# The seven-expert search counted by TensorE, the weights' second halves made on VectorE, and one expert to a turn in the smaller rounds

## The chip, the cores and the metric

The kernel runs on one NeuronCore of a Trainium2 chip. The metric is the device time of one execution in microseconds (us); lower is better. The engines are named as in the profile: PE is TensorE (PEld its weight loads), DVE is VectorE, ACT is ScalarE, POOL is GpSimd, SP the queue of plain DMAs.

## The reference

Three stages follow each other: a two-dimensional Fourier transform, a mixture of eight experts with a greedy assignment, and a dense feed-forward layer.

```
X = fft(fft(x, axis=1), axis=2).real            # x is 8 x 3072 x 256
logits = X.reshape(24576, 256) @ w_gate         # 8 experts, each takes at most 3072 tokens
for (token, e) in order of falling logits:
    if token is free and e is not full: assign token to e
out[tokens of e] = relu(X[tokens of e] @ w1[e]) @ w2[e]
result = (max(h, 0) + alpha * min(h, 0)) @ w_out    with h = out @ w_in
```

## The kernel before

The transform runs first (the first 445 us). It leaves the transformed rows in DRAM (`XD`) and the logits in SBUF (`LG`, 128 partitions x 192 columns x 8 experts).

The greedy assignment is worked out in **rounds**. Each round finds the expert that fills up first, and with it the logit at which it does: a search over a 32-bit key, the upper 16 bits first and the lower 16 after. The tokens that this expert has won are written to a list, the logits of the remaining experts are moved together (`place`), and the next round goes on with one expert fewer. The first list, with all eight experts (`first`, `count_wide`), is made before the feed-forward part starts. Rounds 1 to 7, with n = 7 down to 1 experts, are made while the feed-forward part works on earlier lists.

A search step before (`round`, inner function `search`, L725 to L750) settles two bits. For each of the n experts three DVE instructions (`junk`, L732) count how many of the 192 keys of a partition reach a threshold; one small matmul (`cnt`, L723) sums over partitions; a few DVE instructions choose the digit and subtract it from the keys. Sixteen steps make a search of 32 bits.

The feed-forward part takes 48 **tiles** of 512 tokens, six for each list. A tile is four layers: `l1` (tile name `h`), `l2` (`y`), `l3` (`u`) and `l4` (`o`), the last two one tile behind the first two. PE is given them in 48 **parts** a tile, in a fixed order: eight groups, each of one `l1`, two `l3`, two `l4` and one `l2` part. Every product is made three times with numbers cut into a first half (fp32r) and a remainder, so each part's result is taken from PSUM by ACT (first half) and then DVE (remainder): `hs`, `r` and `g`, `ys`, `xtl`. After each part's matmuls the loop asks the router for its next piece (`next(bg, None)`), and only then emits what takes the part's result out. I call each such call a **turn**: what the router emits in a turn stands on DVE ahead of the part's own remainder. The router's `lag()` lets two turns pass before it puts a matmul on PE. Every engine runs its instructions in this written order.

Before an expert's tiles begin, its eight weight blocks are fetched, and `place_w` cuts each into `wxh` (ACT, L820) and the remainder `wxl` (POOL, L821). Six blocks are placed in the last tile of the expert before, the last two in the first two groups of the expert's own first tile. These first tiles, 6, 12, 18, 24, 30, 36 and 42, are called **switches** below. POOL's queue also holds the gathers of token rows (`xg`) and the scatters of results (`out_dram`).

If a list is not ready when the loop needs it (the gather of the next list's first tile, in group 5 of the tile before), the loop empties turns one after another with no part between them. Round 1 comes to this in tile 5.

Of the kernel before, what the change touches and what calls it, by code (L numbers as in the profile page):

```python
# [10 lines left out]
F32 = mybir.dt.float32  # L11
F32R = mybir.dt.float32r
BF16 = mybir.dt.bfloat16
I32 = mybir.dt.int32
I16 = mybir.dt.int16
U16 = mybir.dt.uint16
F16 = mybir.dt.float16
AF = mybir.ActivationFunctionType
ALU = mybir.AluOpType
AX = mybir.AxisListType  # L20
# [3 lines left out]
P = 128  # L24
B, N, D = 8, 3072, 256
E = 8
TOK = B * N
N1, N2 = 96, 32
NG = 24
HC = 138  # L30
CV = 256
NCOL = TOK // P
# [236 lines left out]
class Router:  # L269
# [395 lines left out]
    def rank(self, n):  # L665
# [24 lines left out]
                yield  # L690
        yield

    def round(self, psum, lists, n):

        nc, wp = self.nc, self.wp
        V = nc.vector
        if n == 1:
            at = wp.tile([P, 2, NCOL], BF16, tag="at", name="at")
            V.tensor_scalar(at[:, 0], self.done, 0.0, None, op0=ALU.is_equal)
            V.memset(at[:, 1], 0.0)  # L700
            V.tensor_copy(self.estar, self.eid[:, :1])
            yield "expert"
            yield from self.place(psum, lists, at, n)
            return
        yield from self.rank(n)
        ke = wp.tile([P, E - 1, NCOL], U16, tag="ke", name="ke")
        s = wp.tile([P, E - 1, 3], BF16, tag="s", name="s")
        junk = [wp.tile([P, NCOL], BF16, tag="w", bufs=2, name="junk") for _ in range(2)]

        def keys(k16):  # L710

            for e in range(0, n, 4):
                m = min(n, e + 4)
                V.tensor_tensor(
                    ke[:, e:m], k16[:, None, :].broadcast_to([P, m - e, NCOL]), self.ohe[:, e:m], op=ALU.mult
                )
                yield

        def total(k):

            cnt = psum(name="cnt")
            cv = cnt[:, : n * k].rearrange("p (e k) -> p e k", e=n)
            nc.tensor.matmul(cv, self.onesb[:, :P], s[:, :n, :k], start=True, stop=True)  # L723
            return cv

        def search():
            step = 65536
            while step > 1:
                step >>= 2
                for e in range(n):  # L730
                    for k in range(3):
                        V.tensor_scalar(  # L732
                            junk[(e + k) % 2], ke[:, e], float((k + 1) * step), 0.0, op0=ALU.is_ge, op1=ALU.add,
                            accum_out=s[:, e, k : k + 1],
                        )
                    if e % 2:
                        yield
                yield from self.lag()
                cv = total(3)
                yield  # L740
                mc = wp.tile([P, 3], F32, tag="mc", name="mc")
                V.tensor_reduce(out=mc, in_=cv.rearrange("p e k -> p k e"), op=ALU.max, axis=AX.X)
                st = wp.tile([P, 3], F32, tag="st", name="st")
                V.memset(st, float(step))
                nk = wp.tile([P, 1], F32, tag="nk", name="nk")
                V.scalar_tensor_tensor(mc, mc, self.CAP, st, op0=ALU.is_ge, op1=ALU.mult, accum_out=nk)
                if step > 1:
                    V.tensor_scalar(ke[:, :n], ke[:, :n], nk, 0.0, op0=ALU.subtract, op1=ALU.max)
                V.tensor_tensor(self.base, self.base, nk, op=ALU.add)
                yield  # L750

        k16 = wp.tile([P, NCOL], U16, tag="k16b", name="k16b")
        V.tensor_scalar(k16, self.hi, 32768.0, 0.0, op0=ALU.add, op1=ALU.max)
        V.memset(self.base, 0.0)
        yield from keys(k16)
        yield from search()
        V.tensor_scalar(self.base, self.base, -32768.0, None, op0=ALU.add)
        key = self.low_key()
        V.memset(self.base, 0.0)
        yield  # L760
        V.tensor_scalar(key, key, 32768.0, None, op0=ALU.add)
        V.tensor_scalar(k16, key, 0.0, 65535.0, op0=ALU.max, op1=ALU.min)
        yield from keys(k16)
        yield from search()

        for e in range(n):
            V.scalar_tensor_tensor(
                junk[e % 2], key, self.base, self.ohe[:, e], op0=ALU.is_ge, op1=ALU.mult, accum_out=s[:, e, :1]
            )
            yield  # L770
        yield from self.lag()
        cv = total(1)
        yield
        we = wp.tile([P, E], F32, tag="we", name="we")
        V.scalar_tensor_tensor(we[:, :n], cv[:, :, 0], self.CAP, self.wE[:, :n], op0=ALU.is_ge, op1=ALU.mult)
        V.tensor_reduce(out=self.wm, in_=we[:, :n], op=ALU.max, axis=AX.X)
        V.scalar_tensor_tensor(
            we[:, :n], we[:, :n], self.wm, self.eid[:, :n], op0=ALU.is_equal, op1=ALU.mult, accum_out=self.estar
        )
        yield  # L780
        at = self.choose(key)
        yield "expert"
        yield from self.place(psum, lists, at, n)
# [6 lines left out]
def ffn_phase(tc, XD, wcat, W3S, alpha, out, router):  # L790
    nc = tc.nc
    with ExitStack() as ctx:
# [25 lines left out]

        def split_w(dh, dl, raw):
            nc.scalar.copy(dh, raw)  # L820
            nc.gpsimd.tensor_sub(dl, raw, dh.bitcast(F32))  # L821

        st = {}

        def new_lists(r):
            lm = lp.tile([P, 2, NG], F32, tag="lm", name=f"lm{r}")
            idx = lp.tile([P, NG], I32, tag="idx", name=f"idx{r}")
            st["lists", r] = (lm, idx)
            return lm, idx
# [19 lines left out]
        def place_w(r, i):  # L849
            split_w(wxh[i], wxl[i], raws.pop((r, i)))  # L850
# [189 lines left out]
        with tc.tile_pool(name="r_first", bufs=1) as fp:  # L1040
            i = None
            first = router.first(psum_r, new_lists(0), fp)
            for tag in first:
# [5 lines left out]
                if tag == "expert":  # L1049
                    expert_idx(0)  # L1050
                    i = 0
# [15 lines left out]
        op = ctx.enter_context(tc.tile_pool(name="m_o", bufs=3))  # L1067
# [166 lines left out]
```

## Time and profile before

| | us |
|---|---|
| median of 3 runs (3885.62 to 3892.1) | 3889.99 |
| the profiled execution | 3883.63 |
| its span, first to last instruction | 3881.9 |
| PE busy | 3788.3 (98%) |
| PEld busy | 3327.8 (86%) |
| DVE busy | 2611.5 (67%) |
| ACT busy | 1815.8 (47%) |
| POOL busy | 657.7 (17%) |

The profiled execution lies 6.4 us under the median. Busy time is the time in which at least one instruction of the engine runs; matmuls overlap, and their ends are modelled, so PE's 98% is no statement on how well it is used. What can be read from it is where PE stands idle.

### The profile page before, as it was taken

The numbers are of one execution on the slowest core, as the hardware profiler recorded it, in microseconds if no ns is written. First come the engines' busy times: TensorE is split into PE (matmuls) and PEld (weight loads), VectorE is DVE, ScalarE is ACT, GpSimd is POOL, SyncE is SP. The second block draws the span as 40 slices with busy tenths as digits, with TensorE's granted clock in tenths as the row PEclk, the third lists the DMA queues.
The fourth block names the chain that finished last, engine by engine and source line by source line (L and its number), as shares of the span: only waits on it lengthen the run. The fifth ranks groups of instructions, "written<-read, shape, count | busy, mean of one in ns | idle before, by whom it ended". The sixth has DMA issues, their size and how long they took to land.

```text
span 3881.9 us, 62378 instructions
## 1 busy us (share of the span) xinstructions
PE 3788.3 (98%) x23666; PEld 3327.8 (86%) x23676; DVE 2611.5 (67%) x7650; ACT 1815.8 (47%) x3455; POOL 657.7 (17%) x905
## 2 busy tenths in 40 slices
PE   9999899999999999999999999999999999999999
PEld 8998587888888788888888888888888888888888
DVE  5776899689868977887877777556444444444444
ACT  4553244444444444454444444454445444544444
POOL 2211300030011110030011110030112201211010
PEclk9999899999999999999999999999999999999999
DMA  8786100010000000010000000010001000100000
GB/s 235 203 218 199 44 12 12 10 40 12 12 23 23 23 23 12 12 44 12 12 23 23 22 23 12 12 44 12 14 20 33 22 12 22 29 16 22 12 17 12
DMA packets 95053, 153.53 MB, mean 40 GB/s; under 512 B 14688, under 2 KB 64544, under 8 KB 94752
## 3 DMA queue, kind: packets, MB, share of 16 engines
q0 software_dynamic: 30400, 90.21, 7.8%
q1 hardware_dynamic: 63440, 58.75, 5.5%
q8 instruction: 185, 3.03, 0.3%
q14 instruction: 116, 0.95, 0.1%
q10 hardware_dynamic: 912, 0.58, 0.1%
HBM read 90.77 MB, written 58.72 MB: 39 GB/s over the span
## 4 chain that ended last, share of the span: by engine, by line
PE 83%; DVE 13%; issue 2%; ACT 1%; DMA 1%; POOL 0%; SPq 0%; ACTq 0%; POOLq 0%; DVEq 0%
PE o L998 24%; PE u L918 23%; PE y L918 12%; PE h L918 11%; DVE junk L732 5%; PE b L209 4%; PE a L150 3%; DVE r L971 2%; PE ls L659 2%; PE c L226 2%; DVE g L976 2%; PE xps L908 1%; DVE hs L932 1%; DMA x<-in_x 1%; ACT r L969 1%
## 5 line engine op out<-in xcount | busy, mean ns | idle before, releaser
L998 PEld LDWEIGHTS o<-w3t,g 128*128 128x128 f32 x9216 | 1178.8, 188 | 92.3 <-DVE g L976 30.7
L998 PE MATMUL o<-w3t,g 128*128 128x256 f32 x9216 | 1209.5, 281 | 27.2 <-DVE g L976 25.2
L918 PE MATMUL u<-ys,w3t 128*128 128x512 f32 x4608 | 1183.7, 394 | 0.2 <-DVE ys L954 0.2
L971 DVE SCALAR_TENSOR_TENSOR r<-a,nal,r 128x512 f32<-128x512 f32 x768 | 597.3, 778 | 623.2 <-ACT a L970 620.7
L918 PEld LDWEIGHTS u<-ys,w3t 128*128 128x128 f32 x4608 | 841.6, 189 | 160.7 <-DVE ys L954 1.2
L969 ACT ACTIVATE r<-u 128x512 f32<-128x512 f32 x768 | 459.4, 598 | 847.9 <-PE u L918 668.4
L1021 POOL DMA_INDIRECT out_dram<-os,orow x192 | 190.0, 989 | 2594.3 <-ACT os L1017 2526.0
L931 ACT ACTIVATE hs<-h 128x512 fp32r<-128x512 f32 x384 | 230.3, 600 | 779.5 <-PE h L918 756.0
L976 DVE TENSOR_TENSOR g<-r,g 128x512 fp32r<-128x512 f32 x768 | 526.7, 686 | 4.3
L932 DVE SCALAR_TENSOR_TENSOR hs<-h,hs 128x512 fp32r<-128x512 f32 x384 | 264.5, 689 | 380.2 <-ACT hs L931 379.9
L918 PE MATMUL y<-hs,wxh 128*128 128x512 f32 x1536 | 490.3, 400 | 0.6 <-DVE hs L932 0.6
L975 ACT CAST g<-r 128x512 fp32r<-128x512 f32 x768 | 477.8, 622 | 22.9 <-DVE r L971 22.9
L970 ACT ACTIVATE a<-u 128x512 f32<-128x512 f32 x768 | 454.9, 592 | 0.0
L732 DVE TENSOR_SCALAR_CACHE_REDUCE junk<-ke 128x192 bf16<-128x192 uint16 x1296 | 367.5, 348 | 0.1
L918 PEld LDWEIGHTS y<-hs,wxh 128*128 128x128 f32 x1536 | 283.9, 189 | 61.2 <-DVE hs L932 1.0
L918 PE MATMUL h<-xth,wxh 128*128 128x512 f32 x768 | 304.0, 396 | 1.9 <-DVE hs L932 1.8
L918 PE MATMUL y<-hs,wxl 128*128 128x512 f32 x768 | 303.6, 395 | 0.0
L918 PE MATMUL h<-xtl,wxh 128*128 128x512 f32 x768 | 301.0, 392 | 0.2 <-DVE xtl L913 0.2
L918 PE MATMUL h<-xth,wxl 128*128 128x512 f32 x768 | 300.1, 391 | 0.0
L892 POOL DMA_INDIRECT xg<-XD,idx x192 | 207.3, 1080 | 85.0 <-issue 55.8
L918 PEld LDWEIGHTS y<-hs,wxl 128*128 128x128 f32 x768 | 144.4, 188 | 35.1
L918 PEld LDWEIGHTS h<-xth,wxl 128*128 128x128 f32 x768 | 144.5, 188 | 32.3
(227 smaller groups left out, 3641.5 us busy)
## 6 DMA issues: line engine op xcount, KB each, us to landing
x<-in_x SPq DMA_DIRECT2D x63, 384.0 KB, 4.8
XD<-xs SPq DMA_DIRECT2D x96, 128.0 KB, 2.8
XD<-xs SPq DMA_DIRECT2D x184, 64.0 KB, 2.7
raw<-in_w POOLq DMA_DIRECT2D x32, 256.0 KB, 4.4
W3S<-hl POOLq DMA_DIRECT2D x32, 256.0 KB, 3.2
w3t<-W3S SPq DMA_DIRECT2D x16, 512.0 KB, 9.6
tw<-in_tw POOLq DMA_DIRECT2D x12, 512.0 KB, 6.1
xg<-XD,idx POOLq DMA_INDIRECT x192, 2.8
```

Of the source, the lines that this page charges most:

```text
L732: V.tensor_scalar(junk[(e + k) % 2], ke[:, e], float((k + 1) * step), 0.0, op0=ALU.is_ge, op1=ALU.add, accum_out=s[:, e, k : k + 1],)
L892: nc.gpsimd.indirect_dma_start(out=x[:, j, :], out_offset=None, in_=XD, in_offset=bass.IndirectOffsetOnAxis(ap=idx[:, j0 + j : j0 + j + 1] ...
L918: nc.tensor.matmul(o, w, a, start=(first and n == 0), stop=(last and n == 2))
L931: nc.scalar.activation(h[:, 0], ps, AF.Relu)
L932: nc.vector.scalar_tensor_tensor(h[:, 1], ps, 0.0, h[:, 0].bitcast(F32), op0=ALU.max, op1=ALU.subtract)
L969: nc.scalar.activation(r, ps, AF.Relu)
L970: nc.scalar.activation(a, ps, AF.Relu, scale=-1.0)
L971: nc.vector.scalar_tensor_tensor(r, a, nal[:, j : j + 1], r, op0=ALU.mult, op1=ALU.add)
L975: nc.scalar.copy(g[:, 0], r)
L976: nc.vector.tensor_sub(g[:, 1], r, g[:, 0].bitcast(F32))
L998: nc.tensor.matmul(o[:, s, :], a, w, start=(j == 0 and n == 0 and s % 2 == 0), stop=(j == 15 and n == 2 and s % 2 == 1), skip_group_check= ...
L1021: ins = nc.gpsimd.indirect_dma_start(out=out, out_offset=bass.IndirectOffsetOnAxis(ap=orow[:, jj : jj + 1], axis=0), in_=os[:, s, :], in_o ...
```

## The change

Three things are changed. In the round with seven experts (round 1) the search is made by a new function, `search_beside`: it settles four bits a step, in eight steps. DVE makes a table of 15 comparisons for every key (`ind`, in three pieces a step), PE counts by multiplying the table with the experts' membership (`d`, 24 matmuls a step), and a last matmul sums (`cnt`). In rounds 3 to 6 (n under 6) the search ends a turn after every expert instead of after every second one. And `wxl` is written by DVE instead of POOL, in every place.

```diff
+    def search_beside(self, psum, n):
...
+                def ind(h):
+                    t = wp.tile([P, H, 16, 8], BF16, tag="ol", bufs=2, name="ind")
...
+                    V.tensor_tensor(
+                        t[:, :, first:k], blocks(key)[:, s, None, :].broadcast_to(sh),
+                        lows[:, i, None, 16 - k + first :, :].broadcast_to(sh), op=ALU.is_ge,
+                    )
+                    inds[h] = t
+
+                def products(h):
+                    t = inds.pop(h)
+                    for c in range(H):
+                        a = (h * H + c) * 8
+                        nc.tensor.matmul(
+                            dv, t[:, c, :k].rearrange("p k j -> p (k j)"), self.ohe[:, :n, a : a + 8],
+                            start=(h + c == 0), stop=(h == 2 and c == H - 1),
+                        )
+
+                ind(0)
+                yield
+                ind(1)
+                yield from self.lag()
+                d = psum(name="d")
+                dv = d[:q, : 8 * n].rearrange("p (e c) -> p e c", e=n)
+                products(0)
+                yield
+                ind(2)
+                products(1)
+                yield
+                yield from self.lag()
+                products(2)
+                yield
+                V.tensor_tensor(dm[:q, :n], dv, self.mske[:q, None, :].broadcast_to([q, n, 8]), op=ALU.mult)
+                s = wp.tile([P, E], F32, tag="we", name="se")
+                V.tensor_reduce(out=s[:q, :n], in_=dm[:q, :n], op=ALU.add, axis=AX.X)
+
+                V.scalar_tensor_tensor(
+                    s2[:q, :n, :k], s[:q, :n, None].broadcast_to([q, n, k]), -1536.0,
+                    self.mskj[:q, None, :k].broadcast_to([q, n, k]), op0=ALU.add, op1=ALU.mult,
+                )
+                yield from self.lag()
+                cnt = psum(name="cnt")
+                cv = cnt[:, : n * k].rearrange("p (e k) -> p e k", e=n)
+                nc.tensor.matmul(cv, self.ones[:q], s2[:q, :n, :k], start=True, stop=True)
+                yield
...
+                V.scalar_tensor_tensor(
+                    mc[:, :k], mc[:, :k], cap, st[:, :k], op0=ALU.is_ge, op1=ALU.mult, accum_out=nk
+                )
+                if i:
+                    nxt = wp.tile([P, NCOL], I16, tag="cur", bufs=2, name="cur")
+                    V.tensor_scalar(nxt, key, nk, -32768.0, op0=ALU.subtract, op1=ALU.max)
+                    key = nxt
+                V.tensor_tensor(self.base, self.base, nk, op=ALU.add)
+                yield
...
     def round(self, psum, lists, n):
...
         yield from self.rank(n)
+        if n == E - 1:
+            key = yield from self.search_beside(psum, n)
+            at = self.choose(key)
+            yield "expert"
+            yield from self.place(psum, lists, at, n)
+            return
...
-                    if e % 2:
+                    if e % 2 or n < 6:
                         yield
...
         def split_w(dh, dl, raw):
             nc.scalar.copy(dh, raw)
-            nc.gpsimd.tensor_sub(dl, raw, dh.bitcast(F32))
+            nc.vector.tensor_sub(dl, raw, dh.bitcast(F32))
```

How the change moves instructions is shown at three places. The first is PE in the search of round 1, tile 2; `cnt`, `d`, `h`, `u`, `y` and `o` are named as above, the numbers tell buffers apart. Before, the only matmul of the search is `cnt`:

```order
L918 MATMUL h_1_7170<-xth_7061,wxl_5171 128x512
L723 LDWEIGHTS onesb
L723 MATMUL cnt<-s,onesb 128x21
L918 MATMUL u_2_7182<-ys_7083,w3t_5148 128x512 x6
L998 MATMUL o_7205<-w3t_5146,g_0_7167 128x256 x12
L918 MATMUL u_3_7224<-ys_7083,w3t_5149 128x512 x6
```

With the change, eight matmuls `d`, each with its own weights, follow a part three times a step:

```order
L765 LDWEIGHTS ones
L765 MATMUL cnt<-lows,ones 128x105
L1043 MATMUL u_6_7356<-ys_7061,w3t_5152 128x512 x6
...
L1043 MATMUL h_4_7433<-xth_7039,wxl_5174 128x512
L735 LDWEIGHTS ind
L735 MATMUL d<-oh,ind 120x56
L735 LDWEIGHTS ind
L735 MATMUL d<-oh,ind 120x56
```

So PE gets 24 groups of eight `d` in round 1 and eight `cnt` instead of sixteen.

The second place is DVE in the same search. Before, runs of `junk` counts stand between the parts' own `hs`, `r` and `g`:

```order
L732 TENSOR_SCALAR junk,s<-ke 128x192 x6
L971 SCALAR_TENSOR_TENSOR r_13_6925<-a_13_6926,nal,r_13_6925 128x512
L976 TENSOR_TENSOR g_12_6930<-r_12_6884,g_12_6930 128x512
L732 TENSOR_SCALAR junk,s<-ke 128x192 x15
L932 SCALAR_TENSOR_TENSOR hs_7_6973<-h_7_6963,hs_7_6973 128x512
```

With the change, a piece of the table or three small instructions stand there:

```order
L725 TENSOR_TENSOR ind<-cur,lows 128x8x120
L1096 SCALAR_TENSOR_TENSOR r_11_6824<-a_11_6825,nal,r_11_6824 128x512
L1101 TENSOR_TENSOR g_10_6829<-r_10_6778,g_10_6829 128x512
L1057 SCALAR_TENSOR_TENSOR hs_6_6865<-h_6_6850,hs_6_6865 128x512
L754 TENSOR_TENSOR lows<-d,mske 120x56
L756 TENSOR_REDUCE se<-lows 120x7
L758 SCALAR_TENSOR_TENSOR lows<-se,mskj 120x7x15
```

So a step's 21 counts are gone from DVE, and three `ind` pieces and the small instructions have come.

The third place is the switch of tile 42. Before, POOL has the last two remainders behind the scatters of the tile before:

```order
L1021 DMA out_dram<-os_1_36927,orow_27922 24576x256
L821 TENSOR_TENSOR wxl_5176<-rawx_6_36644,wxh_5168 128x512
L821 TENSOR_TENSOR wxl_5177<-rawx_7_36723,wxh_5169 128x512
L892 DMA xg_37256<-XD,idx_29259 128x256 x4
```

With the change they stand on DVE, one ahead of each of the first two `hs`:

```order
L1140 COPY os_1_36786<-o_36232 128x512
L946 TENSOR_TENSOR wxl_5176<-rawx_6_36503,wxh_5168 128x512
L1057 SCALAR_TENSOR_TENSOR hs_0_36801<-h_0_36794,hs_0_36801 128x512
L1096 SCALAR_TENSOR_TENSOR r_0_36811<-a_0_36812,nal,r_0_36811 128x512
L1096 SCALAR_TENSOR_TENSOR r_1_36823<-a_1_36824,nal,r_1_36823 128x512
L1101 TENSOR_TENSOR g_0_36828<-r_0_36811,g_0_36828 128x512
L946 TENSOR_TENSOR wxl_5177<-rawx_7_36582,wxh_5169 128x512
L1057 SCALAR_TENSOR_TENSOR hs_1_36840<-h_1_36833,hs_1_36840 128x512
```

So POOL holds no arithmetic on tiles here any more, and DVE has one subtraction more in each group that places a block.

## Rows read from the trace of the kernel before

**Rows 1.** Windows by tiles: length, then busy us of PE, PEld, DVE, ACT, POOL, clock, DMA.
```profile
471.00:689.80 218.80, 206.22 (x1169) 176.04 (x1168) 205.08 (x950) 98.52 (x182) 21.73 (x29) 0.99 0.04 13
689.80:842.30 152.50, 149.72 (x991) 131.18 (x990) 112.68 (x263) 68.86 (x128) 31.00 (x34) 1.00 0.09 25
842.30:1063.20 220.90, 210.29 (x1194) 179.68 (x1192) 196.03 (x858) 100.95 (x187) 29.95 (x38) 0.99 0.05 15
1212.40:1433.40 221.00, 211.03 (x1223) 180.55 (x1222) 193.38 (x782) 104.21 (x193) 45.42 (x52) 0.99 0.08 25
1433.40:2448.90 1015.50, 1008.44 (x6328) 877.41 (x6328) 773.13 (x2485) 472.88 (x874) 162.56 (x200) 1.00 0.07 20
2448.90:2583.90 135.00, 135.00 (x787) 118.81 (x787) 64.40 (x114) 69.45 (x129) 34.01 (x38) 1.00 0.11 32
2583.90:3755.50 1171.60, 1164.65 (x6870) 1023.71 (x6870) 564.75 (x895) 572.58 (x1056) 189.40 (x238) 1.00 0.07 20
```

**Rows 2.** PE's waits over the whole run: total us, times, longest.
```profile
PE o L998 <- DVE g L976: 25.2, 20, 3.1
PE cnt L723 <- DVE junk L732: 21.2, 26, 2.4
```

**Rows 3.** Timeline in round 1's search: start, length, instruction, idle before it.
```profile
509.56 0.35 DVE L732 TENSOR_SCALAR_CACHE_REDUCE junk<-ke 128x192 bf16<-128x192 uint16 x1
...
509.84 0.35 DVE L732 TENSOR_SCALAR_CACHE_REDUCE junk<-ke 128x192 bf16<-128x192 uint16 x1
...
513.05 0.39 PE L918 MATMUL h<-xth,wxl 128*128 128x512 f32 x1
...
514.79 0.18 PE L723 MATMUL cnt<-s,onesb 128*128 128x21 bf16 x1 [1.35 <-DVE junk L732]
...
515.26 0.17 DVE L742 TENSOR_REDUCE mc<-cnt 128x3 f32<-128x21 f32 x1
...
516.16 0.15 DVE L749 TENSOR_TENSOR base<-base,nk 128x1 f32<-128x1 f32 x1
```

**Rows 4.** Timeline at the switch of tile 42.
```profile
3424.67 3.51 DVE L971 SCALAR_TENSOR_TENSOR r<-a,nal,r 128x512 f32<-128x512 f32 x1 [0.61 <-ACT a L970]
...
3425.10 2.52 POOL L821 TENSOR_TENSOR wxl<-rawx,wxh 128x512 fp32r<-128x512 f32 x2
...
3428.83 0.38 PE L998 MATMUL o<-w3t,g 128*128 128x256 f32 x1 [2.42 <-DVE g L976]
```

**Rows 5.** Window just behind that wait, columns as in Rows 1.
```profile
3429.40:3432.80 3.40, 3.40 (x13) 2.94 (x12) 1.35 (x2) 1.06 (x3) 2.79 (x4) 0.50 0.38 112
```

**Rows 6.** PE's waits at the switches of tiles 6, 12, 18 and 24.
```profile
PE o L998 <- DVE g L976: 3.1, 1, 3.1
...
PE o L998 <- DVE g L976: 1.8, 1, 1.8
...
PE o L998 <- DVE g L976: 2.3, 1, 2.3
...
PE o L998 <- DVE g L976: 2.7, 1, 2.7
```

**Rows 7.** Groups by form: count, then busy us and mean ns, idle before.
```profile
L976 DVE TENSOR_TENSOR g<-r,g 128x512 fp32r<-128x512 f32 x768 | 526.7, 686 | 4.3
...
L821 POOL TENSOR_TENSOR wxl<-rawx,wxh 128x512 fp32r<-128x512 f32 x64 | 88.6, 1390 | 193.2 <-ACT wxh L820 192.9
```

**Rows 8.** Timeline: the first list's search (395 us), and a list made in tile 31.
```profile
394.65 1.79 DVE L420 TENSOR_TENSOR ind<-cur,lows 128x960 bf16<-128x960 int16 x3
...
395.53 1.59 PE L425 MATMUL d<-oh,ind 128*120 128x64 bf16 x24
...
2674.59 1.16 PE L659 MATMUL ls<-rr,ol 128*128 128x48 bf16 x16
2675.60 1.63 PE L918 MATMUL u<-ys,w3t 128*128 128x512 f32 x6
2677.06 1.59 PE L998 MATMUL o<-w3t,g 128*128 128x256 f32 x12
```

More of the change, by code (lines that the diff above doesn't have):

```diff
@@ L691, in rank, with blocks, search @@
         yield
+    def search_beside(self, psum, n):
+        nc, wp, V = self.nc, self.wp, self.nc.vector
+        cap = self.CAP - 8 * 1536
+        ke = wp.tile([P, E - 1, NCOL], U16, tag="ke", name="lows")
+        kf = ke.rearrange("p e a -> p (e a)")
+        lows = kf.bitcast(I16)[:, :512].rearrange("p (i k j) -> p i k j", i=4, j=8)
+        dm = kf.bitcast(F32)[:, 256 : 256 + 8 * E].rearrange("p (e c) -> p e c", e=E)
+        s2 = kf.bitcast(F16)[:, 640 : 640 + 16 * E].rearrange("p (e k) -> p e k", e=E)
+        for i in range(4):
+            nc.gpsimd.iota(lows[:, i], pattern=[[1 << 4 * i, 16], [0, 8]], base=-32768, channel_multiplier=0)
+        H = NG // 3
+        def blocks(t):
+            return t.rearrange("p (a b) -> p a b", b=8)
+        def search(key, exact=None):
+            for i in reversed(range(4)):
+                step = 1 << 4 * i
+                last = exact is not None and i == 0
+                k = 16 if last else 15
+                first = 1 if last else 0
+                q = 8 * k
+                inds = {}
+                def ind(h):
+                    t = wp.tile([P, H, 16, 8], BF16, tag="ol", bufs=2, name="ind")
+                    s = slice(h * H, h * H + H)
+                    if last:
+                        V.tensor_scalar(t[:, :, 0, :], blocks(exact)[:, s], self.base, None, op0=ALU.is_ge)
+                    sh = [P, H, k - first, 8]
+                    V.tensor_tensor(
[37 more added lines that the diff above has]
+                yield
+                if last:
+                    return cv
+                mc = wp.tile([P, 16], F32, tag="mc", name="mc")
+                V.tensor_reduce(out=mc[:, :k], in_=cv.rearrange("p e k -> p k e"), op=ALU.max, axis=AX.X)
+                st = wp.tile([P, 16], F32, tag="st", name="st")
+                V.memset(st[:, :k], float(step))
+                nk = wp.tile([P, 1], F32, tag="nk", name="nk")
+                V.scalar_tensor_tensor(
[7 more added lines that the diff above has]
+                yield
+        k16 = wp.tile([P, NCOL], I16, tag="k16b", name="k16b")
+        V.tensor_scalar(k16, self.hi, -32768.0, None, op0=ALU.max)
+        V.memset(self.base, -32768.0)
+        yield
+        yield from search(k16)
+        key = self.low_key()
+        V.tensor_scalar(k16, key, -32768.0, 32767.0, op0=ALU.max, op1=ALU.min)
+        V.memset(self.base, -32768.0)
+        yield
+        cv = yield from search(k16, key)
+        ce = wp.tile([P, E, 16], F32, tag="q1", name="ce")
+        V.tensor_scalar(ce[:, :n], cv, cap, None, op0=ALU.is_ge)
+        ne = wp.tile([P, E], F32, tag="ne", name="ne")
+        V.tensor_reduce(out=ne[:, :n], in_=ce[:, :n], op=ALU.add, axis=AX.X)
+        me = wp.tile([P, 1], F32, tag="me", name="me")
+        V.tensor_reduce(out=me, in_=ne[:, :n], op=ALU.max, axis=AX.X)
+        yield
+        we = wp.tile([P, E], F32, tag="we", name="we")
+        V.scalar_tensor_tensor(we[:, :n], ne[:, :n], me, self.wE[:, :n], op0=ALU.is_equal, op1=ALU.mult)
+        V.scalar_tensor_tensor(self.base, me, -1.0, self.base, op0=ALU.add, op1=ALU.add)
+        V.tensor_reduce(out=self.wm, in_=we[:, :n], op=ALU.max, axis=AX.X)
+        V.scalar_tensor_tensor(
+            we[:, :n], we[:, :n], self.wm, self.eid[:, :n], op0=ALU.is_equal, op1=ALU.mult, accum_out=self.estar
+        )
+        yield
+        return key
```

## The prediction

> **What bounds the kernel now.** I cut the feed-forward part into windows by tiles and read, in each, how long PE stood idle [rows 1]. In tiles 28 and 29, where the router asks for nothing, PE is busy for all of 135.0 us, 67.5 us a tile: an undisturbed tile is limited by PE alone, and DVE works 64.4 us in it, 0.67 us in each of 96 turns. So what PE loses to others is its idle time in the other windows: 12.6 us in tiles 1 to 3 (round 1's search), 2.8 us in tiles 4 and 5 (its list), 10.6 us in tiles 6 to 8 (round 2's search), 10.0 us in tiles 11 to 13 (round 3's), 7.1 us in tiles 14 to 27, 7.0 us in tiles 30 to 46. The reader is to see that PE is 98% busy and still loses some 50 us, in a few places.
>
> Whom it waits for stands in the list of waits [rows 2]: 21.2 us in 26 waits of `cnt` for the counts `junk`, 25.2 us in 20 waits of `l4` for the remainder `g`. Both are DVE's work.
>
> Why DVE is late has two causes. The first is load. One count follows the other after 0.28 us, and the steps that close a count, from `mc` to `base`, take 1.05 us [rows 3]. A part is 67.5/48 = 1.4 us of PE. A step with seven experts is 7 turns, 9.8 us; DVE has 7 x 0.67 of its regular work, 21 x 0.28 of counts and 1.05, 11.6 us: late by 1.8 us a step. Six experts: 10.8 against 9.8. Five: 6 turns, 9.3 against 8.4. Four: 8.4 against 8.4, just on time. The idle windows say the same.
>
> The second is POOL. At the switch of tile 42 one `r` takes 3.51 us on DVE, while POOL makes two `wxl` in 2.52 us; `g` stands behind it, and PE waits 2.42 us for that [rows 4]. Every switch has this wait: 3.1, 1.8, 2.3 and 2.7 us [rows 6], and the 7.0 us of tiles 30 to 46 are the last three [rows 1]. Right behind the wait the granted clock is 0.50 for 3.4 us, the 1.2 GHz level [rows 5]; PE then does half its work and loses another 1.7 us. I found five such stretches in the feed-forward part: behind four switches (6, 12, 30, 42) and behind one wait for counts in tile 3.
>
> **The change, part by part.**
>
> *The remainders on DVE.* Gone are the seven switch waits, 3.1 + 1.8 + 2.3 + 2.7 + 7.0 = 16.9 us, and the four slow stretches behind them, 6.8 us. Added are 64 subtractions on DVE. The nearest row is `g`, the same shape and also from SBUF to SBUF, 0.69 us [rows 7]. In the tiles that place blocks that is one to a group of six turns, and DVE is idle for half of an undisturbed tile [rows 1]: cost nothing, covered by that idle half. The cover is missing where round 2 searches, since DVE has more than it can do there. The written order puts four of them there (two late in tile 5, two early in tile 6): 0 to 2.8 us, I take 1.2. Such a subtraction also waits for ACT's `wxh`; behind it stand the next `hs`, which PE needs only a part later. POOL's next fetch of a weight block now waits for DVE, a few microseconds at most, with three groups (25 us) before the block is used. In the first list, where PE waits for DVE, five subtractions come onto DVE (+3.4 us) and five holds by POOL of up to its 1.39 us [rows 7] go (-7): between -5 and +3, and I take 0.
>
> *Round 1's search.* PE's idle time of 12.6 us and the slow stretch in tile 3 (1.7 us) can go. PE gets 24 x 8 = 192 `d`. The first list has made the same matmul, 24 in 1.59 us or 0.066 us each with the tail of the last one; the router's `ls` comes 16 times in the 1.01 us between its start and the next `u`, 0.063 us [rows 8]. I take 0.060: 11.5 us, all on PE's path; bounds 0 (where PE would have waited anyway) and 12.7. Eight wider `cnt` for sixteen: nothing (from 514.79 the next part starts within a tenth). DVE has, in a step of now 12 turns (16.8 us), 8.0 us of regular work, three `ind` in 1.79 us [rows 8], and closing steps that I estimate at twice the 1.05 us above: some 12 us, so it is on time. I leave 1 us of waits.
>
> *Round 1's list.* The new search takes 95 turns where the old one took 112, so the list is done early in tile 5 by the written order, and no turns are forced there: the 2.8 us go.
>
> *One expert a turn.* A step with five experts becomes 9 turns (12.6 us) with DVE at 6.0 + 4.2 + 1.05 = 11.3 us. Of the 10.0 us in tiles 11 to 13, 1.8 belong to the switch; 8.2 go, and I leave 1. Of the 7.1 us in tiles 14 to 27, 5.0 belong to two switches, 2.1 go. The searches get longer in turns, but each list is still written ahead of its tile by some two tiles' turns or more in the order, so nothing is forced.
>
> *Round 2* keeps its grouping (n is 6), and its 10.6 - 3.1 = 7.5 us stay. It begins some thirty turns earlier; its seven-turn steps meet every place of the six-part group either way.
>
> *What idle time hides.* A matmul of 512 columns is shown 0.39 us long, but the next can start after 0.23: from 513.05 to 514.79 are 1.74 us for a wait shown as 1.35 [rows 3]. So each wait costs about 0.16 us more than the view says. Some 30 of the 46 waits [rows 2] lie outside round 2: 4.8 us.
>
> **The sum.** Gone: 16.9 + 6.8 + 12.6 + 1.7 + 2.8 + 8.2 + 2.1 + 4.8 = 55.9 us. Added: 11.5 (`d`) + 2.0 (left waits) + 1.2 (round 2) = 14.7 us. Net -41 us. Against the profiled execution's 3883.6 us that is 3842.6; the median of the runs shown lies 6.4 us above it, and I predict for such a median: 3890 - 41 = 3849, a little lower for the rounding of my waits, **3848 us**.
>
> The Trainium skill bears on the price of `d`. Its page "TensorE: Matmul & The Clock Gate" says in "Weight-path perf modes — Fast Weight Load (FWL) and DoubleRow" that fast loading needs weights of exactly 128 columns, and in "LDWEIGHTS (loading the stationary operand)" that a load otherwise takes columns/1.2 ns; with 120 columns that would be, as an estimate from the page, 100 ns for each of 168 `d`, 18 us instead of 11.5. The trace does not agree: 24 with 120 columns came in 1.59 us [rows 8].
>
> **Rivals.**
>
> *VectorE becomes the bound at the switches* (chance 0.13). If DVE's subtraction, waiting for ACT, holds `hs` or `g` up by its own length in each of the 56 places of the seven switches, PE loses up to 56 x 0.69 = 38 us; half of that leaves a gain of 22, 3868 us. For it: DVE runs strictly in order, and `g` was late by exactly such a hold. Against it: the hold was 2.5 us, and a part is 1.4 us long.
>
> *The products cost more* (0.08). PE may space `d` by the loading of its weights. The nearest slow row is the `o` part, 12 matmuls in 1.59 us, 0.13 us each [rows 8]: 25 us instead of 11.5, a gain of 27.5, 3862 us. The row of `d` itself speaks against it, but there `d` stood alone and not between parts. The rule of the page above would end near this case.
>
> *The gain is larger* (0.05): round 2's 7.5 us and their hidden part go too, because the earlier search meets other parts: 3838 us or below.
>
> *The small rounds gain nothing* (in the main case's range): if five counting turns in a row make `g` as late as before, 10.3 us stay, 3858 us.
>
> *Slower* (0.04). PE takes the router's matmuls in order. Round 1 now has 32 places where PE can stand before a product that DVE has not yet prepared (24 groups, 8 `cnt`). If each waits as the `cnt` of [rows 3], 1.35 + 0.16 us, that is 48 us, and the kernel ends at 3897 us; at 2.4 us, the longest wait of that kind [rows 2], at 3930. It decides from a mean wait of 1.5 us. Against it: a piece is written three turns, 4.2 us, ahead of its products, and DVE has 12 us of work in 16.8.
>
> **How the numbers follow.** The main case, a gain of 32 to 50 us, has 0.68. A measurement of this kernel can tell 0.2%, about 8 us, from no change; I give 0.02 to ending within that, 0.04 to slower, 0.94 to faster (the main case and the first three rivals). The range goes from the larger gain with cheap products (58 us: 3832) to the dearer products with some waits at the switches (22 us: 3868).
>
> **What would show it.** Right: in tiles 28 to 46 every tile at 67.4 us, no DVE instruction of `r` over 1 us at a switch, the clock at 1.00 through; eight `d` in about 0.5 us between parts in tiles 1 to 3, each part behind them without idle time; waits of `cnt` for `junk` left in round 2 alone. Wrong: idle time of PE before `d` or before the new `cnt`, new waits for `hs` or `g` in the last tile before a switch, `d` spaced by 0.1 us or more, forced turns in later rounds.

## The result, and the profile after

| | before | after |
|---|---|---|
| median, same chip | 3888.94 us | 3841.3 us (3839.86 to 3845.24) |
| ratio, 95% interval | | 0.9879 [0.9862, 0.9896] |
| the profiled execution | 3883.63 us | 3841.6 us |
| POOL busy | 657.7 us (17%) | 569.2 us (15%) |
| DVE busy | 2611.5 us (67%) | 2520.4 us (66%) |

The kernel is 47.6 us faster by the medians, 42.0 us by the two profiled executions; 41 were forecast. Within the profiled pair 40.2 us lie in tiles 1 to 46; the rest is a tile 0 that begins 3.9 us earlier and takes 1.5 us longer, which, as the start of tile 0 in the other runs shows (below), is mostly chance. The page of the changed kernel, its total and busy times:

```profile
span 3839.6 us, 61993 instructions
...
PE 3789.1 (99%) x23859; PEld 3332.8 (87%) x23859; DVE 2520.4 (66%) x7024; ACT 1817.9 (47%) x3455; POOL 569.2 (15%) x845
```

PE is as busy as before, 0.8 us more, in a span that is 42.3 us shorter: on balance, what went is idle time. The windows show where, cut at the same tiles as [rows 1], but for the last cut, which is at the start of tile 32 here and of tile 30 there (after the length come the busy times of PE, PEld, DVE, ACT and POOL, then the granted clock):

```profile
468.70:685.00 216.30, 216.08 (x1398) 187.34 (x1397) 136.54 (x305) 99.14 (x183) 21.85 (x29) 1.00 0.04 13
685.00:836.10 151.10, 147.93 (x949) 128.61 (x948) 116.69 (x331) 68.47 (x127) 20.96 (x28) 1.00 0.08 25
836.10:1059.10 223.00, 215.51 (x1253) 183.98 (x1252) 187.12 (x790) 101.54 (x188) 26.16 (x36) 0.98 0.05 15
1204.10:1408.40 204.30, 204.30 (x1193) 177.25 (x1191) 165.09 (x665) 103.57 (x191) 33.94 (x44) 1.00 0.09 27
1408.40:2402.50 994.10, 993.98 (x6151) 868.17 (x6150) 733.09 (x2345) 473.52 (x873) 140.31 (x184) 1.00 0.06 20
2402.50:2701.50 299.00, 299.00 (x1982) 261.63 (x1981) 210.97 (x527) 136.91 (x253) 44.32 (x56) 1.00 0.07 22
2701.50:3713.10 1011.60, 1011.60 (x5882) 890.19 (x5881) 469.33 (x699) 506.19 (x932) 147.33 (x196) 1.00 0.07 21
```

In tiles 1 to 3, 12.6 us of idle time have become 0.2; in tiles 11 to 13, 10.0 have become none; from tile 14 on, 0.1 us is left of 14.1. Only tiles 4 to 8 still lose: 3.2 and 7.5 us. Tiles 1 to 3 are nevertheless only 2.5 us shorter, since PE now works there on `d`. The list of PE's waits, whole run, answers to [rows 2]:

```profile
PE o L1123 <- DVE g L1101: 5.8, 8, 1.7
...
PE cnt L848 <- DVE junk L857: 3.4, 8, 1.3
...
PE o L1123 <- DVE r L1096: 1.7, 1, 1.7
```

Of 46.4 us in 46 waits, 10.9 in 17 are left, and 9.9 of them lie in tiles 5 to 8, where round 2 searches. The switch of tile 42, which answers to [rows 4]:

```profile
3386.35 0.75 DVE L1096 SCALAR_TENSOR_TENSOR r<-a,nal,r 128x512 f32<-128x512 f32 x1 [0.61 <-ACT a L1095]
3387.01 0.68 DVE L1101 TENSOR_TENSOR g<-r,g 128x512 fp32r<-128x512 f32 x1
3387.09 1.47 POOL L1017 DMA_INDIRECT xg<-XD,idx  x1 [0.30 <-issue]
...
3387.62 0.69 DVE L946 TENSOR_TENSOR wxl<-rawx,wxh 128x512 fp32r<-128x512 f32 x1
```

`r` takes 0.75 us instead of 3.51, `g` follows on time, and the remainder comes after it at 0.69 us, as the row of `g` [rows 7] had it. PE in round 1's new search, tile 2:

```profile
556.56 0.57 PE L735 MATMUL d<-oh,ind 128*120 128x56 bf16 x8
556.97 0.48 PE L1043 MATMUL h<-xth,wxh 128*128 128x512 f32 x1
```

Eight `d` push the next part back by 556.97 - 556.56 = 0.41 us, 0.051 us each, and no wait stands ahead of them. In the last of the eight steps the table has 16 comparisons and so 128 columns instead of 120, and there eight `d` push the next part back by 0.22 us (tile 3):

```profile
642.30 0.38 PE L735 MATMUL d<-oh,ind 128*128 128x56 bf16 x8
642.52 1.65 PE L1123 MATMUL o<-w3t,g 128*128 128x256 f32 x12
```

The granted clock, which [rows 5] shows at 1.2 GHz behind a wait:

```profile
851.40:854.80 3.40, 3.40 (x14) 2.92 (x13) 2.81 (x9) 1.08 (x3) 1.27 (x3) 0.51 0.27 77
926.50:929.80 3.30, 3.30 (x12) 2.62 (x11) 2.16 (x8) 0.56 (x2) 1.05 (x2) 0.50 0.27 79
```

Five such stretches in tiles 1 to 46 have become two, both in round 2.

### The profile page after: what moved, and what is told of

It is laid out like the page before. It is cut to its first block, busy times and chain, and to the rows that moved or that the text cites. A ratio compares the mean times of both kernels' runs of the same rounds, so it can differ in the third digit from the quotient of the medians.

```text
span 3839.6 us, 61993 instructions
## 1 busy us (share of the span) xinstructions
PE 3789.1 (99%) x23859; PEld 3332.8 (87%) x23859; DVE 2520.4 (66%) x7024; ACT 1817.9 (47%) x3455; POOL 569.2 (15%) x845
## 4 chain that ended last, share of the span: by engine, by line
PE 92%; DVE 5%; issue 1%; DMA 1%; ACT 1%; POOL 0%; SPq 0%; another core or an unknown queue 0%; POOLq 0%; ACTq 0%; DVEq 0%
PE o L1123 26%; PE u L1043 26%; PE y L1043 13%; PE h L1043 13%; PE b L209 4%; PE a L150 3%; PE ls L659 2%; PE c L226 2%; DVE junk L857 2%; PE xps L1033 1%; DMA x<-in_x 1%; DVE r L1096 1%; DVE g L1101 1%; PE warm L1159 1%; PE d L425 0%
## 5 line engine op out<-in xcount | busy, mean ns | idle before, releaser
L1096 DVE SCALAR_TENSOR_TENSOR r<-a,nal,r 128x512 f32<-128x512 f32 x768 | 576.2, 750 | 650.4 <-ACT a L1095 613.1
L857 DVE TENSOR_SCALAR_CACHE_REDUCE junk<-ke 128x192 bf16<-128x192 uint16 x960 | 275.8, 347 | 0.1
L1043 PEld LDWEIGHTS h<-xth,wxl 128*128 128x128 f32 x768 | 144.2, 188 | 32.1
```

The costliest lines, as they stand in the source:

```text
L857: V.tensor_scalar(junk[(e + k) % 2], ke[:, e], float((k + 1) * step), 0.0, op0=ALU.is_ge, op1=ALU.add, accum_out=s[:, e, k : k + 1],)
L1043: nc.tensor.matmul(o, w, a, start=(first and n == 0), stop=(last and n == 2))
L1096: nc.vector.scalar_tensor_tensor(r, a, nal[:, j : j + 1], r, op0=ALU.mult, op1=ALU.add)
```

## The experiments

Each row's ratio is to the kernel before, run in the same job. "Tiles" below are lengths from the first transposing matmul of a tile to that of the next, worked out from the traces; an undisturbed one is 67.44 us. The transform ends some us earlier or later from one execution to the next (tile 0 began at 440.6 to 448.0 us), so where 4 us or less are at stake, the tiles decide and not the whole time.

| run | edit | median, us | ratio, 95% interval |
|---|---|---|---|
| only_wxl | before, remainders on DVE | 3851.77 | 0.9908 [0.9892, 0.9925] |
| only_beside | before, new search in round 1 | 3889.83 | 1.001 [1.0, 1.002] |
| only_turns | before, one expert a turn in rounds 3 to 6 | 3870.56 | 0.9956 [0.9939, 0.9972] |
| turns6 | after, one expert a turn in round 2 too | 3826.96 | 0.984 [0.9823, 0.9856] |
| pool_sub | after, two idle subtractions on POOL per switch | 3871.39 | 0.9955 [0.9938, 0.9971] |
| pool_copy | the same with two idle copies | 3848.74 | 0.9897 [0.988, 0.9914] |
| beside6 | after, new search in round 2 too | 3841.96 | 0.9878 [0.9861, 0.9894] |
| no_beside | turns6 without the new search | 3834.68 | 0.986 [0.9843, 0.9876] |
| beside_1turn | only_beside, round 3 begins 1 turn later | 3879.29 | 0.9986 [0.9976, 0.9995] |
| beside_4turns | only_beside, round 3 begins 4 turns later | 3882.56 | 0.9996 [0.9987, 1.0006] |
| before2 | before again, one run | 3884.75 | |

**Each part alone.** First the remainders:

```diff
-            nc.gpsimd.tensor_sub(dl, raw, dh.bitcast(F32))
+            nc.vector.tensor_sub(dl, raw, dh.bitcast(F32))
```

> The kernel before with the remainders wxl on VectorE and nothing else. Theory (GpSimd's subtractions hold VectorE up at the switches): the seven switch waits (16.9 us) and the slow-clock stretches behind them (6.8 us) go and nothing comes back, a gain of 25 us against the kernel before, 3864 us; no r over 1 us at a switch. Rival (the subtractions become a load of VectorE's own): a gain of 10 to 15 us, with new waits for hs or g in the last tile before a switch.

Measured: 35.0 us faster by the medians (29 to 42 by the interval), 32.1 by the profiled executions. The seven switch tiles are 4.0, 3.0, 2.6, 2.7, 4.0, 2.7 and 4.3 us shorter, 23.2 in all: the switches' waits and their slow stretches, 23.7 in my sum. Tiles 5 and 11 are 4.6 us shorter together, which the sum lacked: POOL also made one `wxl` there every six turns while DVE was full, in tile 11 with counts, in tile 5 with the list of round 1. POOL in tile 11, and DVE in tiles 11 and 5, before:

```profile
1239.21 1.43 POOL L821 TENSOR_TENSOR wxl<-rawx,wxh 128x512 fp32r<-128x512 f32 x1 [6.75 <-ACT wxh L820]
...
1239.62 1.04 DVE L746 SCALAR_TENSOR_TENSOR mc<-mc,st 128x3 f32<-128x3 f32 x1
...
802.20 1.45 DVE L650 TENSOR_TENSOR eq<-lh,ihi 128x192 bf16<-128x192 int16 x1
```

The same `mc` takes 0.16 us in only_wxl, and an `eq` mostly 0.35. PE's waits in tile 11, before:

```profile
PE cnt L723 <- DVE junk L732: 5.3, 6, 0.9
```

and with the remainders on DVE:

```profile
PE cnt L723 <- DVE junk L732: 3.0, 6, 0.6
```

The other 4.5 us of the profiled pair are an earlier start of tile 0; 1.1 of them come from the first list, which is that much shorter. So 29 us, 28.0 in tiles 1 to 46 and 1.1 in the first list, can be placed; the rest of the 35.0 cannot.

Second, `search_beside` for seven experts in the kernel before (the function as in the change, and this call):

```diff
+        if n == E - 1:
+            key = yield from self.search_beside(psum, n)
+            at = self.choose(key)
+            yield "expert"
+            yield from self.place(psum, lists, at, n)
+            return
```

> The kernel before with the seven-expert search on TensorE and nothing else. Theory: round 1's waits (12.6 us idle, 1.7 of slow clock, about 1.5 hidden) and the forced turns in tile 5 (2.8) go, 9.3 us of products come (24 groups at 0.39 us as the changed kernel's trace has them): a gain of 8 to 9 us, 3880 us. Rival (the waits only move to round 2, which starts earlier and now meets the switch of tile 6): a gain of 0 to 3 us, 3887 us.

Measured: 3.0 us slower, with an interval that begins at no change; tiles 1 to 46 are 5.6 us longer, with seven slow stretches for five. Both expectations missed the sign. The tiles say where: 1 to 5 gain 2.2 us, 6 to 10 lose 2.0, 11 to 13 lose 12.0 (tile 11: 81.05 for 74.51, tile 12: 76.46 for 74.63, tile 13: 75.51 for 71.91), 14 to 27 gain 6.1. In tiles 11 to 13 round 3 searches, in which nothing was edited. A step with five experts has six turns there, and a group of parts has six, so every step meets the same part. PE in tile 11, before:

```profile
1237.80 0.17 PE L723 MATMUL cnt<-s,onesb 128*128 128x15 bf16 x1 [0.83 <-DVE junk L732]
...
1247.32 0.18 PE L723 MATMUL cnt<-s,onesb 128*128 128x15 bf16 x1 [0.89 <-DVE junk L732]
...
1256.84 0.18 PE L723 MATMUL cnt<-s,onesb 128*128 128x15 bf16 x1 [0.88 <-DVE junk L732]
```

and with the new search ahead of it:

```profile
1239.10 0.18 PE L848 MATMUL cnt<-s,onesb 128*128 128x15 bf16 x1 [1.69 <-DVE junk L857]
...
1249.43 0.18 PE L848 MATMUL cnt<-s,onesb 128*128 128x15 bf16 x1 [1.69 <-DVE junk L857]
...
1259.76 0.18 PE L848 MATMUL cnt<-s,onesb 128*128 128x15 bf16 x1 [1.69 <-DVE junk L857]
```

Step after step waits twice as long, and the earlier list of round 1 has put the steps behind another part of the group: `cnt` stands behind the second `u` instead of behind `y`. In tile 12, where POOL writes `wxl` in the first two groups alone, the last four steps behind the second `u` wait 0.72 to 0.82 us (the two before them not at all), and those behind `y` in the kernel before 0.03 or less: where the second `u` costs more, it is 0.8 us a step in both tiles. A delay of round 3 by single turns moves the steps along the group again:

```diff
+        if n == 5:
+            for _ in range(1):
+                yield
         yield from self.rank(n)
```

(in beside_4turns `range(4)`; five experts, n = 5, are round 3.)

> The kernel with nothing changed but the TensorE search in round 1 (3890 us), and one empty turn ahead of round 3. A step of round 3 is six turns and a group of the tile six parts, so every step meets the same part; in that kernel cnt stands behind the second l3 and waits 1.85 us in tile 11, in the kernel before behind l2 and waits 1.05. The empty turn puts it behind l2 again. Theory (the place in the group sets the wait of each step): cnt waits about 1.05 us a step in tile 11, tiles 11 to 13 lose 5 to 8 us less, 3883 us. Rival (the loss of that kernel comes from the products themselves): within 2 us of 3890.

> As the kernel with one empty turn ahead of round 3, with four empty turns. By the written order cnt then stands behind the first l3 of a group in nearly all of round 3's steps. In the kernel before, the few steps that stood there (tiles 12 and 13) waited 0.7 us or less. Theory: tiles 11 to 13 lose 8 to 12 us less than with no empty turn, 3880 us. Rival (the place does not matter): within 2 us of 3890.

Measured: one idle turn makes only_beside's 3.0 us loss a 5.7 us gain, with tiles 11 to 13 at 222.3 us for 233.0 (221.0 before), and `cnt` behind `y` again, waiting 0.83 to 0.89 us in tile 11 after a first wait of 1.72. Four turns bring tiles 11 to 13 to 226.4 and the whole to 2.4 us of gain (0.9 by tiles 1 to 46), less than expected: `cnt` stands behind the first `u`, and of six steps there in tile 11 three wait 1.52 to 1.66 us and the others not at all. So the loss was one of place, not of the new search; but the place alone does not fix the wait, and how much a given place costs I could not work out beforehand.

Third, the smaller rounds:

```diff
-                    if e % 2:
+                    if e % 2 or n < 6:
```

> The kernel before with one expert a turn in rounds 3 to 6 and nothing else. Theory (VectorE's load per turn): the 8.2 us of waits in tiles 11 to 13, 2.1 in the later rounds and their hidden part go, a gain of 11 to 13 us, 3877 us; the switch waits stay. Rival (the waits in tiles 11 to 13 come from the switch of tile 12): a gain under 4 us.

Measured: 16.2 us faster by the medians; tiles 1 to 46 are 11.6 us shorter in the profiled pair, although seven slow stretches lie in them and five before, which costs 3.4 us. Tile 11 falls from 74.51 to 67.99 us. The three parts alone add up to -35.0 + 3.0 - 16.2 = -48.2 us by the medians, beside -47.6 for all three together. The tiles do not bear that agreement out: by tiles 1 to 46 it is -28.0 + 5.6 - 11.6 = -34.0 beside -40.2. The new search is worth something else in company; no_beside, below, takes it out of the whole.

**Round 2.** The prediction left it its idle time; so:

```diff
-                    if e % 2 or n < 6:
+                    if e % 2 or n < 7:
```

> The changed kernel with one expert a turn in round 2 (six experts) too. Theory (round 2's waits are VectorE's load per turn): a step becomes 10 turns, 14.1 us of TensorE, with 12.8 us of work on VectorE, and most of what tiles 5 to 8 lose in the changed kernel (some 17 us with two slow-clock stretches) goes: a gain of 12 to 15 us against the changed kernel, 3828 us. Rival 1 (the waits come from the subtractions that now stand in tiles 5 and 6): under 4 us. Rival 2 (the list of round 2 comes too late, its last pieces are forced): no gain or a loss, with waits in tile 11.

Measured: 3826.96 us, 14.3 less than the changed kernel. This is the fastest version here, as expected. Tiles 5 to 8 fall from 296.2 to 273.3 us, and some of it comes back later with the longer search. PE from 9 us into tile 5 to 18 us into tile 9, the stretch in which the changed kernel's round 2 lost most:

```profile
775.00:1058.00 283.00, 283.00 (x1643) 246.68 (x1642) 239.29 (x937) 143.14 (x264) 49.63 (x64) 1.00 0.09 26
```

It is busy throughout, at the full clock, and no `cnt` waits for `junk` any more. The subtractions in tiles 5 and 6 are still there, so the changed kernel's loss in round 2 was the grouping of DVE's counts.

The other way to treat round 2 is to give it the new search too:

```diff
-        if n == E - 1:
+        if n >= E - 2:
```

> The changed kernel with round 2 (six experts) searched on TensorE as well. Theory: what tiles 5 to 8 lose (some 17 us with slow clock) goes, 9.3 us of products come: a gain of 5 to 9 us against the changed kernel, 3834 us, so less than one expert a turn gives there (14.3 us). Rival (the products wait for VectorE or disturb the parts): no gain.

Measured: 0.7 us longer than the changed kernel, so no gain by the medians where 5 to 9 us were expected; without the start of tile 0, 3.7 us later in the profiled pair, its tiles are 2.3 us shorter. That is about what the terms give once they are measured: in tiles 4 to 8 idle time of 10.7 us falls to 2.7 (1.3 of it a `d` that waits for `ind`), two slow stretches (3.4 us) go, and 24 groups of `d` add 9.3: 8.0 + 3.4 - 9.3 = 2.1. The expectation had 17 us to be gone instead of 11.4. So idle time was bought with nearly as much of PE's own time.

**The new search in company.** turns6, with all rounds by the old search:

```diff
-        if n == E - 1:
+        if n == 99:
```

> The kernel with one expert a turn in rounds 2 to 6 and wxl on VectorE, without the TensorE search in round 1. Theory: round 1's waits and its forced turns come back and its products go, 8 us in tiles 1 to 5, and the last turns of round 2's list are forced in tile 11, 1 to 3 us: 9 to 11 us longer than the same kernel with the TensorE search (3827 us), 3837 us. Rival (the TensorE search is worth nothing, as alone): 3827 us or less.

Measured: 7.7 us longer than turns6 by the medians, 9.6 in the tiles (8.3 without tile 0); 9 to 11 were expected. So the new search is worth some 8 us when the rounds after it do not care about their place in the group, and in the kernel before, where they do, nothing or a loss.

**Is it POOL's subtraction?** In the changed kernel two instructions of POOL are added, one behind each of the first two `place_w` of a switch tile; they write into a buffer that nobody reads:

```diff
+                    nc.gpsimd.tensor_sub(spare[0].bitcast(F32R), spare[0], wxh[5].bitcast(F32))
```

and in pool_copy

```diff
+                    nc.gpsimd.tensor_copy(spare[0], wxh[5].bitcast(F32))
```

> The changed kernel, with two idle subtractions on GpSimd (128x512, into a buffer that nobody reads) added at each of the seven switches, where the two wxl stood on GpSimd before. No other engine waits for them. Theory (a GpSimd subtraction holds VectorE's instruction while it runs): at every switch one r or g takes over 2 us, TensorE waits about 2.4 us, some waits are followed by a slow-clock stretch: 17 to 28 us longer than the changed kernel, 3858 to 3869 us. Rival (the waits before came from the order behind wxl in GpSimd's queue, or from wxl's readers): within 3 us of the changed kernel.

> As the kernel with two idle subtractions on GpSimd at each switch, but with two copies (one input) instead. If any GpSimd instruction on SBUF holds VectorE for its own length, r is held for the length of the two copies; I estimate 0.5 to 0.8 us each by the one-input copies of LG (16 columns in 0.28 us) and the subtraction (1.26 us), so 0 to 8 us longer than the changed kernel. If only GpSimd instructions with two inputs hold it, no instruction of VectorE is lengthened and the time is the changed kernel's.

Measured against the changed kernel: the subtractions cost 30.1 us (4 of them a later start of tile 0) where 17 to 28 were expected, the copies 7.4 (3.3 of them the start) where 0 to 8 were. The hold comes back with the subtraction alone, though DVE has all its other work as in the changed kernel. The switch of tile 42 in pool_sub:

```profile
3411.20 2.35 DVE L1100 SCALAR_TENSOR_TENSOR r<-a,nal,r 128x512 f32<-128x512 f32 x1 [0.61 <-ACT a L1099]
...
3411.68 2.99 POOL L1238 TENSOR_TENSOR rawx<-rawx,wxh 128x512 fp32r<-128x512 f32 x2
...
3413.47 1.75 DVE L1105 TENSOR_TENSOR g<-r,g 128x512 fp32r<-128x512 f32 x1
...
3415.27 1.85 PE L1127 MATMUL o<-w3t,g 128*128 128x256 f32 x10 [2.33 <-DVE g L1105]
```

`r` and `g` are stretched as in [rows 4], and PE waits 2.33 us. In pool_copy:

```profile
3393.03 0.96 DVE L1100 SCALAR_TENSOR_TENSOR r<-a,nal,r 128x512 f32<-128x512 f32 x1 [0.61 <-ACT a L1099]
...
3393.48 2.01 POOL L1238 COPY rawx<-wxh 128x512 f32<-128x512 f32 x2
...
3393.92 1.09 DVE L1105 TENSOR_TENSOR g<-r,g 128x512 fp32r<-128x512 f32 x1
...
3395.07 1.44 PE L1127 MATMUL o<-w3t,g 128*128 128x256 f32 x10 [0.29 <-DVE g L1105]
```

Here `r` takes 0.2 us more, `g` 0.4, and PE waits 0.29. The Trainium skill bears on it: its page "SBUF — State Buffer", in "Who interferes with whom", says that a DVE instruction with two inputs in SBUF contends with a GpSimd instruction that reads SBUF, and that the ports the two share are an exclusive lock. That `r` and `g` are the ones stretched agrees. Two things agree less: `r` begins 0.48 us before the first subtraction and is stretched all the same, and the copies, which read SBUF too, lengthen DVE by a part of their own time only, while their own times spread from 0.63 to 1.09 us.

**How steady is the kernel before?**

> The kernel before once more, for a second profile. Theory (the slow-clock stretch behind a wait of some 2.4 us comes in some executions and not in others): the waits at the switches stand at the same times and lengths within 0.1 us, and the number of slow stretches in the feed-forward part differs from five by one to three, 1.7 us of span each. Rival (which waits are followed by a slow stretch is fixed by the kernel): the same five.

Measured: 3884.75 us, with other slow stretches than in the first trace: six of them instead of five, one twice as long (6.8 us). In the first, PE waits 2.29 us at the switch of tile 18 and 2.42 at that of tile 42; behind the first of them it goes on at full clock, with 21 matmuls in 3.4 us, and behind the second with 13, at half the clock [rows 5]:

```profile
1735.00:1738.40 3.40, 3.40 (x21) 2.82 (x20) 2.81 (x7) 1.31 (x3) 2.79 (x3) 1.00 0.40 116
```

In the second trace the waits are 2.30 and 2.43 us, and it is the other way round, tile 18 slow and tile 42 not:

```profile
1734.00:1737.40 3.40, 3.40 (x14) 3.17 (x15) 3.33 (x10) 1.44 (x3) 2.49 (x4) 0.53 0.28 84
3431.80:3435.20 3.40, 3.40 (x21) 2.96 (x20) 1.59 (x3) 2.15 (x5) 2.60 (x3) 1.00 0.33 92
```

So my count of four slow switches belonged to that execution; the seven waits are the kernel's.

## Why the prediction was right, step by step

Over tiles 1 to 46 the sum of 41.2 us met 40.2, and the places were the forecast ones. That the terms come out so close is partly luck: the remainders gave 5.5 us more than their term and `d` cost 2.2 less, while round 2 took back 2.9 us of idle time and two slow stretches.

- **The remainders on DVE**: right in mechanism, and nothing new waits for them: PE has no idle time left in tiles 28 to 46. Too small, -22.5 in the sum with the 1.2 us added for round 2, 28.0 measured alone in tiles 1 to 46 (35 by the medians). Missing were the 4.6 us in tiles 5 and 11: I looked for POOL's hold only where two fell in a row, and in these two tiles it stretches no `r` or `g` but small instructions such as `mc` and `eq`. The first list, taken at 0, gained 1.1.
- **Round 1's search**: the idle time went as said (12.4 of 12.6 us, one slow stretch of 1.7), and `d` cost 9.3 us for 11.5, 21 groups at 0.41 and 3 at 0.22: the row of the first list was the nearer one, and its tail was in my 0.060. The price that the Trainium skill's page "TensorE: Matmul & The Clock Gate", in "LDWEIGHTS (loading the stationary operand)", gives for a load, columns/1.2 ns, would have made it 18, an estimate, and does not hold here: eight loads of 120 columns and their matmuls took 0.41 us. But the page's distinction, which the prediction cites, shows, and I had not looked for it: eight with 128 columns took 0.22. Tables of 16 comparisons in every step would by that row cost 24 x 0.22 = 5.3 us of PE (an estimate; no run has them). The number of columns alone does not decide it: `ls` has weights of 128, which lie apart in their tile, and came every 0.063 us [rows 8]. The net, some 8 us with turns6, needs the later rounds to be free of their place in the group.
- **Round 1's list**: wrong in its cause. In only_wxl the list is forced as before, and of the 2.8 us only 0.7 are left: 2.1 were POOL's hold on DVE and not the forced turns. The turns went too, but the 2.8 us did not show in the changed kernel: tiles 4 and 5, which now hold the beginning of round 2's search, wait 3.2 us.
- **One expert a turn**: rounds 3 to 6 wait no more. The sum had 8.2 + 2.1 less 1 for a wait left, and some hidden time; 16.2 was measured alone by the medians, 11.6 in tiles 1 to 46, with 3.4 us of more slow stretches against it. Idle time fell by 10.3 us there, in 13 waits; with the prediction's 0.16 us for each, 2.1, some 2.6 us stay open.
- **Round 2 stays**: the step that went wrong in size. It was to keep 7.5 us of idle time, whatever its place; it has 10.7 us in tiles 4 to 8 and two slow stretches, 3.4 us. "Its seven-turn steps meet every place of the six-part group either way" was taken for enough to keep the waits. In only_wxl, where the remainders are on DVE and the search begins as before, tiles 6 to 8 wait 7.9 us, so most of the 3 us more came with the earlier start; which step of the search they belong to was not taken apart. Both slow stretches stand right behind a long single wait, 1.74 and 1.75 us.
- **What idle time hides**: 4.8 us were forecast, 0.16 for each of 30 waits. In tiles 1 to 46 idle time fell by 38.7 us and slow stretches by 5.1, `d` added 9.3, and 40.2 were gained: that leaves 5.7 us for 33 waits fewer, 0.17 each, if nothing else is in it.
- **The median**: I took 41 us from the median of before and expected after's median as far above its profiled run. It was not: 3841.3 beside 3841.6, while before's lie 5 us above. That fits slow stretches that come and go in before (five and six in two traces), with few such waits left after; this is argued from the traces, not shown run by run, and the start of tile 0, which moves by up to 7 us, would do as well.
- **The signs**: most of those for right came: no `r` over 0.76 us, eight `d` in 0.41 us, waits of `cnt` for `junk` in round 2 alone, the clock at 1.00 in tiles 28 to 46. But only tiles 32 to 46 take 67.44 us; tiles 28 to 31 take 72.4 to 77.3, because with longer searches lists (`ls`) are made in all four of them, without idle time. Of those for wrong one came in part: tile 5, the last before a switch, waits 1.6 us for `g`. In turns6, with the same subtractions, it does not, so that was the counts.

None of the rivals came. DVE did not become the bound at the switches, no `d` waited for `ind`, and the products were cheaper than my price.

## What to carry to other kernels

When an engine off the critical path holds up another one's instructions, the price is in the neighbour's rows: look for one instruction of the usual form that takes three times its usual time, the small ones too (`mc` 1.04 us for 0.16), and look at every place where the two meet, not only where the wait is long. Background work that is written in steps of as many turns as the foreground has parts in a group keeps its place for a whole search, so an edit ahead of it can double or remove a wait in code that it never touched; steps that are spread thin enough not to wait anywhere (one expert a turn) make later edits worth what they should be. And before idle time is bought with work on the bounding engine, price that work in its own rows: beside6 removed 11.4 us of loss with 9.3 us of matmuls, and these at 120 weight columns, which cost here nearly twice as much as 128.

## What was not expected of the hardware

The same wait of PE (2.29 and 2.30 us, 2.42 and 2.43) is followed by a stretch of 3.4 us at the 1.2 GHz level in one execution and not in another; behind waits of 1.74 and 1.75 us it came too. Eight `d` take 0.22 us with weights of 128 columns and 0.41 with 120, while `ls`, also with 128, comes every 0.063 us; why these differ stays open. Copies with one input on POOL take 0.63 to 1.09 us beside DVE's two-input instructions and lengthen `r` and `g` by 0.2 to 0.4 us, where subtractions stretch them by 1.1 to 1.6 in pool_sub. Whether the copies and DVE take turns within an instruction stays open.
